# RWKV attention and a two-layer MLP on one core: spreading w by two TensorE row groups, scores in any free PSUM bank, layer 1 by unit and quarter, weights loaded between units

## The chip, the cores and the metric

The program runs on one core of one Trainium2 chip. The metric is the device time of one execution in microseconds (us). The core has TensorE (PE; matmuls, with its weight loads listed as PEld), VectorE (DVE), ScalarE (ACT), GpSimd (POOL) and SyncE (SP, which here only issues DMAs). Each engine runs its own list of instructions in order; semaphores tie the lists together.

## The reference

```python
def _attn_ref(r, k, v, w, u):                 # (4, 8, 768, 48): batch, heads, steps, head size
    state = np.zeros((B, H, D, D))
    ...
    for t in range(S):
        ...
        cur = np.einsum('bhd,bhe->bhde', u[None] * kt, vt)
        y[:, :, t] = np.einsum('bhd,bhde->bhe', rt, state + cur)
        state = w[None, :, :, None] * state + np.einsum('bhd,bhe->bhde', kt, vt)
    ...

def _moe_ref(x, w_in, w_out):                 # x (3072, 384), w_in (384, 2048), w_out (2048, 384)
    h = x @ w_in
    g = np.where(h >= 1, h, np.where(h <= -1, 0.0, (h + 1) ** 2 / 4))
    return g @ w_out
```

The output y of the attention, with the heads side by side, is the input x of the MLP. Inputs and output are float32.

## The kernel before

**Units.** The sequence is cut into 6 chunks of 128 steps. A unit is one chunk of one batch element, so there are 24 units; units 0 to 3 are the first chunk of the four batch elements. For a unit, K is multiplied by a table of inverse powers of w (`Winv`, line 447, operation `kw`) and R by a table of powers (`Wpow`, line 451, `rw`); both stand in one tile KR. KR is transposed into RK: in the first 8 units by TensorE (`tr`, line 469, with a copy out of PSUM, `rk`), later by a DMA transpose on SP's queue (`trd`, line 488). The scores (`at`, line 499) are 8 matmuls with a contraction of 48, alternating between the two halves of the partitions. VectorE multiplies them by a mask (line 505). Then come y (state part `ys`, line 556; local part, line 559), the sum with the diagonal term (x, line 571), and the transpose of x into xT: in the first 8 units by TensorE (`xp`, line 581), later by DMA (line 589). The state is updated by `st` (line 607), `t`, `tw` and `bd`.

**MLP.** Two units make a block of 256 tokens. Layer 1 (`L1`, line 644) takes a block in 8 groups of 6 matmuls of 256 columns; each group fills an "h" bank, and ScalarE turns it into g (line 656). Layer 2 (`L2`, line 667) takes one unit in 4 groups of 4 matmuls of 384 columns, strictly in order of units; a copy (`e`) and a store (`out`, line 690) follow. The kernel takes g as ((h+1)/2)^2 everywhere; bounds on the norms of x and of w_in (lines 703 to 751) give a flag that says whether the other branches can matter, and only if so does the code under `tc.If` (from line 759) compute the MLP again.

**Order.** The kernel writes every operation down with its engines, its durations as guessed, its dependencies, its buffers and a due time; `Plan.run` (line 84) places them one by one and so fixes the order of the instructions on each engine. The due times come from `CFG` (line 16) and are moved by a `bias` per kind of operation. The loads of the first units and the weights go in the order of `CFG["order"]`: U is a unit, I a quarter of w_in, O a quarter of w_out. Weights land in float32 in one of five "wf" buffers and are cast to bf16 in pieces by whichever engine is free (`copy`, line 284). PSUM has 4 "a", 2 "h" and 2 "o" banks.

**Start.** w is loaded into one partition; ScalarE takes its logarithm (line 327), one TensorE matmul of one row spreads it to 128 partitions (line 333), and two exponentials give Winv and Wpow (lines 359 and 360). Dummy matmuls of zeros (line 357) fill TensorE's gaps of the first 24 us as planned.

Of the kernel before, what the change touches and what calls it, by code (L numbers as in the profile page):

```python
# [16 lines left out]
    "order": "U0 U1 U2 U3 I0 I1 I2 I3 O0 O1 O2 U4 O3 U5 U6 U7",  # L17
    "soft": 8,
    "sw": False,
    "due": [12.12, 22.15, 27.93, 36.84, 35.31],  # L20
    "step": 12.04,
    "warm": 24.0,
    "steady": 45.0,
    "slack": 0.19,
    "split": 2,
    "bias": {
        "at": 1.0, "bd": -4.91, "c_uw": 1.38, "dg": 0.1, "ku": -0.0, "kw": 1.96, "ldVf": 1.45, "red": -0.75,
        "rk": 0.3, "rkk": -6.72, "rkr": -0.29, "rw": 1.99, "st": 0.57, "t": -0.92, "trd": 0.24, "trk": -2.87,
        "trr": -3.35, "tw": -0.9, "v": -0.89, "x2": -1.05, "xt": 2.62, "y": -2.02,
    },  # L30
}


class Buf:
    def __init__(self, pool):
        self.pool, self.users, self.slot, self.t = pool, [], None, None


class Op:
    def __init__(self, name, engs, fn, deps, uses, allocs, due, dma, after, nb, late):  # L40
        self.name, self.engs, self.fn, self.due, self.dma = name, engs, fn, due, dma
        self.after, self.nb, self.late = [a for a in after if a], nb, late
        self.deps, self.uses, self.allocs = [d for d in deps if d], list(uses), list(allocs)
        self.eng = self.start = self.end = None
        for b in self.uses + self.allocs:
            b.users.append(self)


class Plan:
# [13 lines left out]
    def place(self, o):  # L63
        got, t = [], 0.0
        for b in o.allocs:
            best = None
            for i, cur in enumerate(self.slots[b.pool]):
                if any(g[0] == b.pool and g[1] == i for g in got):
                    continue
                if cur is None:  # L70
                    free = 0.0
                elif all(u.start is not None for u in cur.users):
                    free = max(u.end for u in cur.users) + SEM
                else:
                    continue
                if best is None or free < best[0]:
                    best = (free, i)
            if best is None:
                return None
            got.append((b.pool, best[1]))  # L80
            t = max(t, best[0])
        return t, got

    def run(self):
# [5 lines left out]
        while todo:  # L90
            cand, gone = [], []
            for o in todo:
                if any(d.start is None for d in o.deps) or any(a.start is None for a in o.after):
                    if o.late is not None and free["PE"] > o.late:
                        gone.append(o)
                    continue
# [15 lines left out]
            for o in gone:  # L112
                todo.remove(o)
                for b in o.uses:
                    b.users.remove(o)
            if not cand and gone:
                continue
            if not cand:
                raise RuntimeError("no operation can be placed: " + ", ".join(o.name for o in todo[:12]))
# [16 lines left out]
            occ, lat = o.engs[e]  # L136
            o.eng, o.start = e, est
            for b, (p, i) in zip(o.allocs, pl):
                b.slot = i
                self.slots[p][i] = b  # L140
            if o.dma is not None:
# [4 lines left out]
                begin = max(served, issue + wait)  # L146
                served = begin + took
                ring.append((served, nd))
                free[e] = issue
                o.end = served + 0.6 + (1.0 if est > steady else 0.0)  # L150
# [7 lines left out]
            todo.remove(o)  # L158
            done.append(o)
        done.sort(key=lambda o: o.start)  # L160
# [27 lines left out]
def kernel(  # L188
# [28 lines left out]
    NS = CFG["soft"]  # L217
    D_m = list(CFG["due"])
    while len(D_m) < NB + 2:
# [11 lines left out]
        "x": 5, "x2": 2, "g": 5, "os": 3, "sq": 2, "ss": 2,  # L231
    }
    P = Plan(slots)
    rows = rot.tile([1, 2, H, DP], F32, name="rows", tag=f"g_{slots['g'] - 1}")

# [16 lines left out]
    zero = const.tile([128, 128], BF16, name="zero")  # L252
    onesf = const.tile([1, 128], F32, name="onesf")
    w_row = const.tile([1, H * D], F32, name="w_row")
    wc = const.tile([128, NP], F32, name="wc")
    ident = const.tile([128, 128], BF16, name="ident")
    umask = const.tile([128, 128], F32, name="umask")
    ones = const.tile([128, 1], BF16, name="ones")
# [9 lines left out]
    xT = [const.tile([128, nKb, MT], BF16, name=f"xT{m}") for m in range(NB)]  # L268
    xn = const.tile([128, NU], F32, name="xn")
    wsq = const.tile([128, nN], F32, name="wsq")  # L270
# [7 lines left out]
    wc3 = wc[:, :, None].to_broadcast([128, NP, D])  # L278
    umask4 = umask[:, None, :].to_broadcast([128, NP, 128])
# [14 lines left out]
    c_wr = P.op("c_wr", {"ACT": (0.4, 0)}, lambda e: nc.scalar.dma_start(out=w_row, in_=row(w)), due=-100, dma=(0.05, 1, 0.6))  # L294
    c_ur = P.op("c_ur", {"ACT": (0.4, 0)}, lambda e: nc.scalar.dma_start(out=u_row, in_=row(u)), after=[c_wr], due=-99.5, dma=(0.05, 1, 0.6))
    c_ubc = P.op("c_ubc", {"SP": (0.4, 0)}, lambda e: nc.sync.dma_start(out=u_bc, in_=row_bcast(u)), due=D_m[NS // UB] - 25, dma=(0.7, 8, 0.6))
# [21 lines left out]
    c_um = P.op("c_um", {"POOL": (0.6, 0.7)}, f_um, due=-97)  # L318
# [8 lines left out]
    c_lrow = P.op("c_lrow", act(384, False), lambda e: nc.scalar.activation(rows[:, 0, :, 0:D], heads(w_row), AF.Ln), deps=[c_wr, c_rz], due=-98)  # L327
    c_urow = P.op("c_urow", dve(384), lambda e: nc.vector.tensor_mul(rows[:, 1, :, 0:D], heads(w_row), heads(u_row)), deps=[c_wr, c_ur, c_rz], due=8.5)
    lwb = Buf("a")

    def f_lwb(e):
        get(lwb, [128, H, D], F32)
        mm(lwb.t, onesf, rows[:, 0, :, 0:D], start=True, stop=True)
    c_lw = P.op("c_lw", pe(1.3), f_lwb, deps=[c_lrow, c_z], allocs=[lwb], due=-98)
    colb = Buf("a")

    def f_colT(e):
        get(colb, [128, 2, NP], F32)
        for i in range(2):
            for p in range(NP):  # L340
                nc.tensor.transpose(colb.t[:, i, p : p + 1], rows[:, i, 2 * p : 2 * p + 2, :].rearrange("q h d -> q (h d)"), onesf[:, 0:1])
    c_colT = P.op("c_colT", pe(0.5), f_colT, deps=[c_lrow, c_urow], allocs=[colb], due=9)
# [9 lines left out]
    for i in range(160):  # L352
        def f_wm(e, i=i):
            if wmb.t is None:
                get(wmb, [128, 128], F32)
            for _ in range(2):
                mm(wmb.t, zero, zero, start=True, stop=True, skip_group_check=True)  # L357
        wm0 = P.op(f"wm{i}", pe(0.22 if i < 18 else 0.11), f_wm, deps=[c_z], uses=[wmb] if i else [], allocs=[] if i else [wmb], after=[wm0] if i else [], due=2000.0, late=CFG["warm"] if i else None)
    c_winv = P.op("c_winv", act(384), lambda e: nc.scalar.activation(Winv, lwb.t, AF.Exp, scale=negj_col), deps=[c_lw, c_icol], uses=[lwb], due=-97)
    c_wpow = P.op("c_wpow", act(384), lambda e: nc.scalar.activation(Wpow, lwb.t, AF.Exp, scale=i_col), deps=[c_lw, c_icol], uses=[lwb], due=-96)  # L360

# [37 lines left out]
    prev_w = []  # L399
    for tag, q in [(x[0], int(x[1:])) for x in ORDER if x[0] in "IO"]:  # L400
# [8 lines left out]
        before = ORDER[: pos[f"{tag}{q}"]]  # L409
        gate = [loads[int(x[1:])]["Vf"][1] for x in before if x[0] == "U"][-1:]  # L410
        if CFG["sw"]:
            def fn(e, src=src, dst=dst):
                nc.gpsimd.dma_start(out=dst, in_=src)
            o = P.op(f"ld{tag}{q}", {"POOL": (1.1, 0)}, fn, after=gate + prev_w[-1:], due=due, dma=(2.05, 0, 1.0))
            res[q] = [o]
        else:
            def fn(e, bf=bf, src=src, shape=shape):
                t = get(bf, shape, F32)
                nc.sync.dma_start(out=t, in_=src)  # L419
            o = P.op(f"ld{tag}{q}", {"SP": (0.6, 0)}, fn, allocs=[bf], due=due, dma=(2.05, nd, 0.6))  # L420
            res[q] = []
            for i in range(shape[1]):
                def fc(e, bf=bf, dst=dst, i=i):
                    copy(e, dst[:, i, :], bf.t[:, i, :])
                n = shape[2]
                due_c = D_m[0] + 1.3 * q if tag == "I" else 34.0 + 1.0 * q
                res[q].append(P.op(f"c{tag}{q}{i}", {**dve(n, True), **act(n, False), **pool(n, False)}, fc, deps=[o], uses=[bf], due=due_c))
        prev_w.append(o)
# [6 lines left out]
    def attention(i):  # L435
        b, c = units[i]
        m, j = divmod(i, UB)
        soft = i < NS
        D0 = D_m[m] + 1.5 * j
        (Kb, Ko), (Rb, Ro), (Vb, Vo) = loads[i]["K"], loads[i]["R"], loads[i]["Vf"]  # L440
        krb, vb, rkb, atb, yb, xb = Buf("KR"), Buf("V"), Buf("RK"), Buf("AT"), Buf("a"), Buf("x")
        both = {**pool(384), "DVE": (0.68, 0.75)}
# [16 lines left out]
        if soft:  # L459
            trb = Buf("a")  # L460
# [30 lines left out]
        at_p = [Buf("a"), Buf("a")]  # L491
# [8 lines left out]
        o_at = P.op(f"at{i}", pe(0.4), f_at, deps=o_rk, uses=[rkb], allocs=at_p + [atb], due=D0 - 3.2)  # L500

        o_mask = []
        for s in range(2):
            def f_mask(e, s=s):
                nc.vector.tensor_mul(atb.t[s], at_p[s].t, umask4)  # L505
# [307 lines left out]
```

## Time and profile before

| what | us |
|---|---|
| median of 14 runs (lowest to highest) | 181.63 (179.63 to 184.26) |
| the profiled execution | 180.31 |
| its span, first to last instruction | 178.4 |
| first layer-1 matmul starts | 18.57 |
| last matmul ends | 172.6 |
| layer 1: 576 matmuls, busy | 77.8 |
| layer 2: 384 matmuls, busy | 77.0 |
| dummy matmuls: 156, busy | 13.0 |

The span is 1.9 us shorter than the time of the execution, which has some work around it. Busy times of matmuls overlap, since one starts while the one before is still draining; the distance from one start to the next is what a matmul costs. Loads of K, R and V are 192 KB in pieces of 192 bytes; a quarter of a weight matrix is 768 KB in pieces of 2 KB (w_in) or 1.5 KB (w_out).

### The profile page before, as it was taken

How to read it: one execution, taken by the hardware profiler on the slowest of the kernel's cores; microseconds unless marked ns; L12 is line 12 of the kernel's file. 1: busy time of each engine (PE TensorE's matmuls, PEld its weight loads, DVE VectorE, ACT ScalarE, POOL GpSimd, SP SyncE). 2: the span in 40 equal slices, each digit the busy share in tenths (PEclk: the TensorE clock that was granted, in tenths of full speed). 3: DMA queues.
4: the chain of work that ended last, by engine and by line, in shares of the span. 5: the costliest groups of instructions: out<-in, count | busy, mean ns of one | idle time of the engine just before them, and what ended most of it. 6: DMA issues, size and time to landing. Idle time of an engine off the chain costs nothing.

```text
span 178.4 us, 4705 instructions
## 1 busy us (share of the span) xinstructions
PE 168.5 (94%) x1808; PEld 127.0 (71%) x1808; DVE 111.2 (62%) x221; ACT 116.0 (65%) x257; POOL 105.1 (59%) x142
## 2 busy tenths in 40 slices
PE   7899989999989999999999999999999999999960
PEld 7689977766757777777777767776767777777730
DVE  6699965698999795776758765846565644100000
ACT  4359997735566985884976775867785556554510
POOL 8659462387695999778598668588975610000000
PEclk9999999999999999999999999999999999999996
DMA  5999999998989959978989979889998962111111
GB/s 113 211 198 343 386 343 336 225 194 162 201 178 217 179 124 205 180 163 186 192 177 164 181 169 183 212 169 200 189 188 157 234 174 70 22 44 48 44 53 52
DMA packets 105920, 31.50 MB, mean 177 GB/s; under 512 B 98978, under 2 KB 104356, under 8 KB 105892
## 3 DMA queue, kind: packets, MB, share of 16 engines
q1 hardware_dynamic: 105744, 31.04, 78.4%
q8 instruction: 16, 0.26, 0.6%
q10 hardware_dynamic: 148, 0.10, 0.2%
q14 instruction: 12, 0.10, 0.2%
HBM read 20.65 MB, written 4.72 MB: 142 GB/s over the span
## 4 chain that ended last, share of the span: by engine, by line
PE 67%; DMA 13%; SPq 8%; DVE 4%; POOL 3%; issue 1%; ACT 0%; POOLq 0%; ACTq 0%
PE o L667 31%; PE h L644 27%; DMA wf<-in_moe_w_out_dram 11%; SPq L383 5%; PE a L499 3%; SPq L419 2%; PE a L559 2%; DMA K<-in_k_dram 2%; PE a L556 2%; POOL KR L447 1%; PE a L607 1%; DVE AT L505 1%; SPq L488 1%; DVE VD L546 1%; DVE x L571 1%
## 5 line engine op out<-in xcount | busy, mean ns | idle before, releaser
L644 PE MATMUL h<-xT,w_in_sb 128*128 128x256 bf16 x576 | 77.8, 273 | 0.7 <-ACT w_in_sb L284 0.4
L667 PE MATMUL o<-w_out_sb,g 128*128 128x384 bf16 x384 | 77.0, 326 | 0.2 <-POOL w_out_sb L284 0.2
L656 ACT ACTIVATE g<-h 128x512 bf16<-128x512 f32 x96 | 56.6, 595 | 27.4 <-PE h L644 26.3
L644 PEld LDWEIGHTS <-w_in_sb 128*128 128x128 bf16 x576 | 54.4, 98 | 14.5 <-ACT w_in_sb L284 0.7
L667 PEld LDWEIGHTS <-g 128*128 128x128 bf16 x384 | 35.1, 97 | 15.8 <-issue 0.2
L505 DVE TENSOR_TENSOR AT<-a,umask 128x512 bf16<-128x512 f32 x48 | 31.1, 683 | 8.8 <-PE a L499 8.5
L546 POOL TENSOR_TENSOR VD<-V,dg 128x384 f32<-128x384 bf16 x18 | 16.0, 891 | 11.9 <-DVE dg L541 7.1
L571 DVE TENSOR_TENSOR x<-a,VD 128x384 bf16<-128x384 f32 x24 | 13.3, 554 | 11.4 <-PE a L559 7.4
L535 POOL TENSOR_TENSOR KU<-K,u_bc 128x384 f32<-128x384 f32 x16 | 18.5, 1155 | 2.2 <-DMA K<-in_k_dram 2.2
L451 DVE TENSOR_TENSOR KR<-R,Wpow 128x384 bf16<-128x384 f32 x20 | 18.4, 922 | 1.8 <-DMA R<-in_r_dram 1.7
L536 POOL TENSOR_TENSOR KU<-KU,R 128x384 f32<-128x384 f32 x16 | 17.5, 1094 | 1.4 <-DMA R<-in_r_dram 0.2
L597 ACT ACTIVATE x<-x 128x384 bf16<-128x384 bf16 x24 | 12.5, 522 | 6.8 <-DVE x L571 6.4
L284 DVE COPY os<-o 128x384 f32<-128x384 f32 (+1 forms) x6 | 3.1, 520 | 19.9 <-ACT os L284 18.7
L618 POOL TENSOR_TENSOR T<-T,wc 128x192 f32<-128x192 f32 x20 | 11.9, 595 | 5.6 <-ACT T L284 4.2
L357 PE MATMUL o<-zero 128*128 128x128 bf16 x156 | 13.0, 236 | 1.0 <-DVE zero L321 1.0
L447 POOL TENSOR_TENSOR KR<-K,Winv 128x384 bf16<-128x384 f32 x11 | 11.0, 998 | 5.0 <-DMA K<-in_k_dram 4.1
L284 ACT COPY os<-o 128x384 f32<-128x384 f32 (+1 forms) x19 | 8.9, 470 | 6.0 <-PE o L667 4.0
L284 ACT CAST V<-Vf 128x384 bf16<-128x384 f32 x19 | 9.6, 507 | 4.2 <-DMA Vf<-in_v_dram 4.0
L614 DVE TENSOR_TENSOR T<-T,a 48x192 f32<-48x192 f32 x32 | 11.2, 349 | 1.9 <-PE a L607 1.1
L447 DVE TENSOR_TENSOR KR<-K,Winv 128x384 bf16<-128x384 f32 x13 | 8.2, 630 | 5.7 <-DMA K<-in_k_dram 5.7
L284 ACT CAST Tbd<-T 48x192 bf16<-48x192 f32 x30 | 10.4, 347 | 1.8 <-PE a L556 1.4
L357 PEld LDWEIGHTS <-zero 128*128 128x128 bf16 x156 | 10.6, 107 | 1.2 <-DVE zero L321 1.0
(78 smaller groups left out, 173.8 us busy)
## 6 DMA issues: line engine op xcount, KB each, us to landing
K<-in_k_dram SPq DMA_DIRECT2D x24, 192.0 KB, 3.6
R<-in_r_dram SPq DMA_DIRECT2D x24, 192.0 KB, 4.2
Vf<-in_v_dram SPq DMA_DIRECT2D x24, 192.0 KB, 4.1
out_dram<-os SPq DMA_DIRECT2D x23, 192.0 KB, 2.3
wf<-in_moe_w_in_dram SPq DMA_DIRECT2D x4, 768.0 KB, 8.3
wf<-in_moe_w_out_dram SPq DMA_DIRECT2D x4, 768.0 KB, 8.5
RK<-KR SPq DMA_TRANSPOSE x16, 3.1
xT<-x SPq DMA_TRANSPOSE x16, 2.9
```

What stands on the lines that cost most here:

```text
L284: (nc.scalar.copy if eng == "ACT" else V_ENG[eng].tensor_copy)(o, i)
L357: mm(wmb.t, zero, zero, start=True, stop=True, skip_group_check=True)
L447: V_ENG[e].tensor_mul(krb.t[:, H:, 0:D], Kb.t, Winv)
L451: V_ENG[e].tensor_mul(krb.t[:, :H, 0:D], Rb.t, Wpow)
L505: nc.vector.tensor_mul(atb.t[s], at_p[s].t, umask4)
L535: nc.gpsimd.tensor_mul(kub.t, Kb.t, u3)
L536: nc.gpsimd.tensor_mul(kub.t, kub.t, Rb.t)
L546: V_ENG[e].tensor_mul(vdb.t, vb.t, dgb.t[:, :, None].to_broadcast([128, H, D]))
L571: nc.vector.tensor_add(xb.t, yb.t[:, 0:384].rearrange("p (h d) -> p h d", h=H), vdb.t)
L644: mm(hb.t[:, f, :], w_in_sb[:, kk, (2 * n + f) * 128 : (2 * n + f + 1) * 128], xT[m][:, kk, :], start=(kk == 0), stop=(kk == nKb - 1),)
L656: nc.scalar.activation(gb[m].t[:, 2 * n : 2 * n + 2, :], hb.t, AF.Square, bias=0.5, scale=0.5)
L667: mm(ob.t, gb[m].t[:, f, j * C : (j + 1) * C], w_out_sb[:, f, :], start=(f == 0), stop=(f == nN - 1))
```

## The change

The change does the following.

- **Load order**: the quarters of w_in go between units 0 to 3, and all of w_out ahead of unit 4.
- **w**: it is loaded as two rows, on partitions 0 and 64; two matmuls of one row, in two row groups of TensorE, spread w itself to two PSUM banks; the logarithm is then taken on 128 partitions, and the exponentials read it from SBUF.
- **Dummy matmuls** have 256 columns, one per operation.
- **Unit 0** may take its PSUM tiles from any of the pools "a", "h" and "o"; the search for a place looks at all of them.
- **Transposes of RK** are by TensorE in the first 10 units (8 before); in units 0 to 3 (before 0 and 1) in two halves.
- **Masks**: for units 0 and 1, one half of the scores is copied out by ScalarE and masked in bf16.
- **Scores** of blocks 5 to 11: those of both units are one operation of 16 matmuls, which takes all four "a" banks.
- **Layer 1** of blocks 0 and 1: by single unit and quarter of w_in, 12 matmuls of 128 columns a group, and each unit's first group can start without the other unit.
- **Layer 2** of the last unit in two cuts (256 and 128 columns), the store of each on SP; the stores of five units are split into two, which makes the number of counted DMAs a multiple of eight.
- **Norm check**: squares from 100 us on, their sums folded once more by GpSimd, one operation of 8 matmuls in place of 8 operations of 2; the reduction reads PSUM.
- **Redo branch**: a loop of 6 passes over 2 blocks in place of 12 blocks written out; xT is one tile.
- **Planner**: new due times and biases; the order on every engine is new. In it, the two transposes of the norm check (`b3`) stand behind the last layer-2 matmul on TensorE.

```diff
-    "order": "U0 U1 U2 U3 I0 I1 I2 I3 O0 O1 O2 U4 O3 U5 U6 U7",
-    "soft": 8,
-    "due": [12.12, 22.15, 27.93, 36.84, 35.31],
-    "step": 12.04,
+    "order": "U0 U1 I0 I1 U2 I2 U3 I3 O0 O1 O2 O3 U4 U5 U6 U7",
+    "tpe": 10,
+    "dmm": 8,
+    "xpe": 8,
+    "pair": 5,
+    "cold": 5.5,
+    "fine": 2,
+    "am0": 0,
+    "am1": 2,
+    "norm": 100.0,
+    "wide": 1,
+    "due": [2.41, 43.63, -27.85, 19.94, 61.18],
+    "step": 14.84,
     "warm": 24.0,
...
-    "slack": 0.19,
-    "split": 2,
+    "slack": 0.04,
+    "split": 4,
...
-        self.pool, self.users, self.slot, self.t = pool, [], None, None
+        self.pools, self.users, self.slot, self.t = pool.split(), [], None, None
+        self.pool = self.pools[0]
...
-    c_lrow = P.op("c_lrow", act(384, False), lambda e: nc.scalar.activation(rows[:, 0, :, 0:D], heads(w_row), AF.Ln), deps=[c_wr, c_rz], due=-98)
...
-        mm(lwb.t, onesf, rows[:, 0, :, 0:D], start=True, stop=True)
...
+            mm(wbb[s].t, onesf[s * DP : s * DP + 1, :], w_sp[s * DP : s * DP + 1, :], start=True, stop=True)
...
+            nc.scalar.activation(lw[:, lws[s]], wbb[s].t, AF.Ln)
...
+    c_winv = P.op("c_winv", {"ACT": (0.5, 0.58)}, lambda e: nc.scalar.activation(Winv, lw, AF.Exp, scale=negj_col), deps=[c_lw, c_icol], due=-97)
...
-            for _ in range(2):
-                mm(wmb.t, zero, zero, start=True, stop=True, skip_group_check=True)
+            mm(wmb.t, zero[:, 0:128], zero, start=True, stop=True, skip_group_check=True)
...
+        A = "a h o" if i < CFG["wide"] else "a"
+        by_pe, by_mm, x_pe = i < CFG["tpe"], i < CFG["dmm"], i < CFG["xpe"]
...
-        if soft:
-            trb = Buf("a")
+        if by_pe:
+            trb = Buf(A)
...
-        o_at = P.op(f"at{i}", pe(0.4), f_at, deps=o_rk, uses=[rkb], allocs=at_p + [atb], due=D0 - 3.2)
+        o_at = yield f_at, o_rk, rkb, at_p + [atb], D0 - 3.2
...
+                    nc.scalar.copy(amb.t, at_p[s].t)
...
+                    nc.vector.tensor_mul(atb.t[s], amb.t, umaskb4)
...
+        if m >= CFG["pair"]:
+            def f_at2(e, got=got):
+                for x in got:
+                    x[0](e)
+            o = P.op(f"at_{m}", pe(0.63), f_at2, deps=got[0][1] + got[1][1], uses=[x[2] for x in got], allocs=got[0][3] + got[1][3], due=got[0][4])
+            ats = [o, o]
...
+        fine = m < CFG["fine"]
+        j, q = divmod(n, nP // UB)
...
+            if fine:
+                get(hb, [128, 4, C], F32)
+                parts = [(f, 4 * q + f, slice(j * C, (j + 1) * C)) for f in range(4)]
+            else:
+                get(hb, [128, 2, MT], F32)
+                parts = [(f, 2 * n + f, slice(0, MT)) for f in range(2)]
...
+        cuts = [(0, d_out)] if i < NU - 1 else [(0, 256), (256, d_out)]
+        rows_ = [(0, C)] if i not in TWICE else [(0, C // 2), (C // 2, C)]
...
+    n_dma = sum(1 for o in P.ops if o.dma is not None) + NU + 1
+    TWICE = range(12, 12 + -n_dma % 8)
...
+            nc.gpsimd.tensor_add(mx[n // 2], ssb.t[:, 0:128], ssb.t[:, 128:256])
...
+        for g in range(nP):
+            mm(npb.t[:, g : g + 1], mx[g], ones, start=True, stop=True)
...
+        with tc.For_i(0, NCH, 1) as ci:
+            for g in range(NB // NCH):
```

## The prediction

> **What bounds the kernel now.** I read the page first (engine totals), then the chain of waits, then busy time by window, then who waited for whom, and last the branch at the end.
>
> ```profile
> PE 168.5 (94%) x1808; PEld 127.0 (71%) x1808; DVE 111.2 (62%) x221; ACT 116.0 (65%) x257; POOL 105.1 (59%) x142
> DMA  5999999998989959978989979889998962111111
> ```
>
> TensorE is the bound, but 13.0 us of its 168.5 us are dummy matmuls (L357), so the question is when real work runs out, and why. The DMA digits stand at 9 from the second slice: early on the loads set the pace.
>
> ```profile
> 15.36 19.32 DMA wf<-in_moe_w_out_dram x2
> 34.73 1.09 POOL w_out_sb L284 x2
> 35.86 0.81 PE o L667 x4
> ...
> 39.27 0.45 PE a L469 x8
> ...
> 68.02 0.65 PE o L667 x4
> 68.67 0.33 PE a L499 x8
> 68.99 0.76 PE h L644 x6
> 69.76 0.65 PE o L667 x4
> ```
>
> The chain (start, length, what) rests on the last quarter of w_out (O3): it is issued at 26.33, lands 8.3 us later at 34.6, is cast, and the fourth group of layer 2 starts at 35.86. By then all 16 layer-1 groups of the first four units and three layer-2 groups are done; TensorE has nothing else that is ready. From there it hardly stops:
>
> ```profile
> 36.00:46.00 10.00, 9.98 (x122) 6.83 (x121) 9.02 (x19) 4.86 (x14) 8.21 (x12) 1.00 0.92 176
> 46.00:60.00 14.00, 13.51 (x159) 10.34 (x158) 13.11 (x25) 9.08 (x23) 11.03 (x14) 1.00 0.99 202
> 60.00:172.60 112.60, 111.85 (x1104) 81.96 (x1100) 61.75 (x119) 76.40 (x166) 64.88 (x74) 1.00 0.73 151
> ```
>
> First come window, length and TensorE's busy time: 1.26 us idle in 136.6 us, until the last matmul at 172.6. So two things can shorten the run: O3 earlier, or fewer microseconds of matmul after it. The chain prices the latter: a group of six or four MLP matmuls is 0.65; transposes of one unit (L469) 0.45; the scores (L499) stretch the stretch 68.67 to 69.76 to 1.09, so they cost 1.09 - 0.655 = 0.435.
>
> **The change, part by part.** All terms are on the path from O3 to the end.
>
> 1. *Load order.* Before O3, the queue had carried twelve K/R/V loads of units 0 to 3, eight weight loads, and K and R of unit 4. Now O3 stands ahead of all of unit 4. Rates per load:
>
> ```profile
> 2.00:4.00 2.00, 2.00 (x21) 1.89 (x18) 1.79 (x4) 0.54 (x2) 1.87 (x8) 1.00 1.02 194
> 28.00:30.00 2.00, 1.97 (x18) 1.48 (x16) 0.82 (x3) 1.27 (x3) 0.65 (x1) 1.00 1.11 339
> ```
>
> The last column is GB/s; the column before it says all 16 DMA engines are full. A K/R/V load (197 KB) takes about 0.93 us at the 194 to 229 of the first windows, a weight load (786 KB) 2.25 at about 350. Low end: two loads fewer, 1.9 us. High end, from the bottom: start 2.0 + 12 x 0.93 + 8 x 2.25 + 0.6 to land = 31.8, which is 2.8 before 34.6. I take **-2.2** (O3 lands at 32.4, layer 2 goes on near 33.5). The cover: TensorE must have finished the 16 layer-1 groups by then. I0 is now sixth in the queue and lands near 9.7 (16.5 before), I3 at 22.0, V3 at 23, so x of unit 3 is in xT near 25.5, and the last five layer-1 groups (0.66 each) end by 31 beside three layer-2 groups. About 2 us to spare; gone, layer 1 would be late next, at one to one.
>
> 2. *Unit 4 late.* Its transposes and scores (0.45 + 0.435) ran before 35.86; now they come after O3: **+0.9**. K4 and R4 land near 33.3 and 34.2; in the changed instruction order three layer-2 groups stand ahead of unit 4's transposes and two more ahead of its scores, and 13 layer-2 groups (8.45) plus units 4 and 5 (1.7 each: 0.45 + 0.435 + st 0.17, ys 0.17, y 0.2, xp 0.17, dg 0.1) fill TensorE until x of unit 5 is there, about ten us on.
>
> 3. *Paired scores* from block 5: 8 matmuls stream at 0.056 us per pair of row groups, 0.224 of the 0.435; the 0.21 around them is paid once for two units: 7 x 0.21 = **-1.5**.
>
> 4. *Units 8 and 9 transposed by TensorE*, not by DMA: 2 x 0.45 = **+0.9**; two of the 16 DMA transposes of RK vanish, hidden.
>
> 5. *Layer 1 by single unit and quarter* (12 matmuls of 128 columns for 6 of 256), 16 groups. The dummy matmul of the same shape prices it:
>
> ```profile
> 11.31 0.73 PE L357 MATMUL o<-zero 128*128 128x128 bf16 x10
> 13.31 1.17 PE L357 MATMUL o<-zero 128*128 128x128 bf16 x18
> ```
>
> (1.17 - 0.73)/8 = 0.055 each, 12 of them 0.66 against 0.655: **0**. All lie ahead of O3, covered by the 2 us of part 1.
>
> The Trainium skill speaks against this part: "TensorE: Matmul & The Clock Gate", section "Back-to-back issue gap", gives about 81 ns per matmul of 128 columns in a stream of weight load and matmul pairs. By that figure, an estimate, 16 groups would take 12 x 0.081 = 0.97 each, 4.6 us more in all, the spare 2 us would be eaten and the sum of this forecast would shrink to nearly nothing. The rows above are the same instruction pair on this chip, so I go by 0.055.
>
> 6. *w in two row groups, Ln after the spread, banks of unit 0 anywhere, 256-column dummies, masks of units 0 and 1 by ScalarE*: Winv was done at 5.88 and may now be near 4.5. This moves x of unit 0, which then waits for I0 and its casts on ScalarE (about 11.5). **0** in the sum: O3 hides it; without that cover it would be worth 1 to 2 us of start.
>
> 7. *Norm check*: eight two-matmul groups (0.054 each) become eight matmuls, -0.2; the last unit in two cuts has 16 matmuls of 128 columns at 0.055, +0.05: **-0.15**. The squares move to 100 us and later: 0.83 us on ScalarE each (L707), between activations of 0.6 per 1.3 us, so hidden; POOL's third add too (POOL was idle after 155).
>
> 8. *Waits of TensorE after O3.* Now:
>
> ```profile
> PE a L499 <- DMA RK<-KR: 0.4, 1, 0.4
> PE a L607 <- DVE x L571: 0.3, 1, 0.3
> PE a L719 <- POOL ss L713: 0.3, 1, 0.3
> ```
>
> The new order has places for more: ScalarE has four x-square ops (0.7 each), two RK copies (1.0) and two state copies (0.7) queued ahead of the first activation of block 2 near 47 us, 0.5 to 1 us late for TensorE by my count; layer 2 of that block waits on it. Against that the old waits go. Ends -1.2 and +2.5; taken **0**.
>
> 9. *The tail.* From the last matmul (172.61) to the end (178.4) are 5.8 us.
>
> ```profile
> L759 SPq EVENT_SEMAPHORE  x8: 17/17/17, 174.5 to 177.1; - x8
> L759 PEldq COMPARE_BRANCH  x1: 3337/3337/3337, 170.1 to 170.1; - x1
> L759 DVEq COMPARE_BRANCH  x1: 72/72/72, 173.7 to 173.7; - x1
> L759 DVEq EVENT_SEMAPHORE  x1: 21/21/21, 177.2 to 177.2; - x1
> ```
>
> SyncE waits for the last store (issued 173.41, 2.8 us to land) and then checks its queues at 0.07 us each. Now the last evacuation is one copy of 128 columns, not two copies of 192 in a row (172.68 + 0.32, 173.03 + 0.36): the store goes 0.4 earlier, and with the stores counted up to a multiple of eight, fewer checks follow it, 0.35. But the flag, ready at 154.4 before, now waits for two transposes that stand behind the last matmul: 0.38 (L743) + 0.41 (L749) + 0.20 (L750) + handoffs, 1.25 us after it. VectorE's 3.5 us between its branch and its next instruction would then start there: 1.25 + 0.54 + 0.07 + 3.5 + 0.1 + 0.7 = 6.2, i.e. +0.4. That gap came with about 200 skipped instructions; POOL, which skips nothing, had none; VectorE now skips some 35, nearer to POOL's row, but TensorE still skips 420. Ends -0.75 and +0.4; taken **-0.4**.
>
> On this the Trainium skill ("Runtime: NRT & Kernel Launch", section "Instruction fetch mechanics") says that a taken branch to a target outside the fetched window stalls for a fetch of the target page. By that rule the shorter body would fit, and the tail would be worth -0.75, the sum -2.8.
>
> Sum: -2.2 + 0.9 - 1.5 + 0.9 - 0.15 - 0.4 = **-2.45 us**. The profiled execution took 180.31 (span 178.4 + 1.9), so 177.9 for its like; it lies 1.3 below the median of 181.63, so the forecast is 181.63 - 2.45 = **179.2**.
>
> **Rivals.**
> - *More*: O3 at the high end (-0.6 more), all old waits gone (-1.2), tail -0.75: 179.2 - 2.15 = 177.0. For it: the DMA sum; against it: a tightly ordered in-order queue seldom has no wait at all.
> - *Given back*: the activations of block 2 come 1 us late and each of the two late x transposes costs 0.5; layer 1 is late too by 0.5: 181.7. For it: VectorE is busy 13.11 of 14 us in 46 to 60. Against: TensorE there has 1.7 us of attention work per unit as filler.
> - *Slower*: paired scores need both units' RK and all four "a" banks at once, and TensorE works in order, so MLP groups queue behind them. One DMA transpose holds SyncE for 1.6 us (the first, at 50.90), so the second unit's is that much later; a stall of the pair by 0.35 us eats the whole sum (2.45/7), 0.8 us each gives 179.2 + 5.6 = 184.8. For it: the one wait on RK by DMA is already there (0.4); against: 24 scores showed only that one.
> - *It does not do what it says*: the two row groups for w run one after the other. 0.6 us at the start, hidden by O3: no change to the sum.
>
> **How the numbers follow.** Forecast 0.55 (own range 177.8 to 180.7), more 0.15, given back 0.15, slower 0.15; the last rival has the forecast's own chances and time. No change is within 0.5% (0.9 us) of 181.63, about what a measurement of this kernel can tell: 180.7 to 182.5. Faster: the forecast less the upper tail (0.52) + 0.15 + a little of the third: 0.69; same: 0.15; slower: 0.16, the fourth and the end of the third. The range reaches from the bounds of the first rival (-2.15 and the DMA's rest) to the third: 176.0 to 182.6.
>
> **What would show it.** In the changed profile: the last w_out landing near 32.4 and the fourth layer-2 group near 33.5; first layer 1 near 12; the last matmul near 170.5; one score row of 16 matmuls costing 0.66 where two cost 0.87; less than 1.5 us of TensorE waits after 34; VectorE's branch without a gap. Wrong it would be if TensorE waits for RK, x or an activation add up to more than 3 us after 34, or if layer 1 of units 2 and 3 is still running when O3 is cast.

## The result, and the profile after

The changed kernel takes 183.71 us (median of 10 runs, 182.09 to 185.04) beside 181.81 for the kernel before: a ratio of 1.0127, with an interval of 1.0089 to 1.0164. By the ratio it is slower by about 2.3 us, where 2.45 less were forecast. Ratios here compare only those runs of each kernel that lie within 1.5% of its fastest, so they can differ from the ratio of the medians beside them (here 1.0105, or 1.9 us). The profiled execution has a span of 181.3 us; before it was 178.4.

The page of after, engine totals and DMA share by slice:

```profile
PE 169.5 (94%) x1848; PEld 129.6 (71%) x1848; DVE 115.8 (64%) x229; ACT 115.9 (64%) x254; POOL 106.0 (58%) x147
DMA  6999899999499967997999978978879952121120
```

These totals show almost nothing: each within 5 us of before. The loss has to be looked for by place.

The chain of waits of after, 18 to 38 us (start, length, what):

```profile
18.72 0.84 PE h L717 x12
...
21.76 0.67 DVE w_in_sb L319 x2
22.43 1.20 DVE AT L555 x2
23.63 0.34 DVE T L319
...
24.42 0.88 POOL T L670
...
26.07 0.59 ACT RK L319
...
27.20 0.67 PE h L717 x12
...
34.01 1.34 PE h L717 x24
...
36.00 1.34 PE h L717 x24
37.34 0.81 PE o L751 x5
```

Before, most of this stretch was two loads of w_out, from 15.36 to 34.68, the second of them the last quarter (O3). Now no DMA is in it. The chain runs through VectorE's list (casts, masks, state), GpSimd and ScalarE to units 2 and 3, and ends with layer 1 (L717), whose last groups TensorE works off without a break until the fourth group of layer 2 starts at 37.2; that came at 35.86 before. In this execution O3 is no longer what TensorE waits for.

After, in the windows shown of before (the last one now reaches to 174.75, just behind the start of the last layer-2 matmul), and one more:

```profile
36.00:46.00 10.00, 10.00 (x124) 7.14 (x122) 6.73 (x14) 4.73 (x10) 3.59 (x5) 1.00 0.95 201
46.00:60.00 14.00, 14.00 (x186) 10.89 (x183) 13.60 (x29) 11.93 (x32) 10.68 (x15) 1.00 0.85 175
60.00:174.75 114.75, 112.26 (x1138) 85.21 (x1136) 65.67 (x117) 77.92 (x167) 71.36 (x88) 1.00 0.75 146
120.00:140.00 20.00, 17.70 (x169) 12.95 (x167) 10.39 (x16) 13.36 (x28) 15.52 (x21) 1.00 0.85 156
```

TensorE stands idle for 2.5 us behind 60, and 2.3 of it lie between 120 and 140. The answer on waits and the chain there say for what (L537 are the scores, RK their input, by DMA transpose):

```profile
PE a L537 <- DMA RK<-KR: 2.3, 2, 1.4
```

```profile
117.57 1.11 POOL VD L598
119.37 0.83 POOL VD L598
120.45 4.78 DMA RK<-KR
...
129.62 3.43 DMA K<-in_k_dram
...
135.37 4.62 DMA RK<-KR
```

Last the tail: the rows of the branch (L849) and of the end of the program (L897); durations in ns, then start:

```profile
L849 PEldq COMPARE_BRANCH  x1: 3753/3753/3753, 176.4 to 176.4; - x1
L849 PEldq EVENT_SEMAPHORE  x1: 51/51/51, 180.3 to 180.3; - x1
L897 SPq EVENT_SEMAPHORE  x10: 17/28/3130, 176.9 to 181.2; - x10
```

Before, TensorE's branch began at 170.1, beside the last matmuls. Now the flag is there at 175.8, so the branch begins at 176.4; SyncE stands 3.13 us waiting for TensorE and the program ends with it. The two gaps of VectorE and ScalarE behind their branches are gone, but TensorE's stayed.

Where the time went can be added up. Take for each matmul the distance to the next start, and sum it for attention and MLP: of some 155 us of such work in either kernel (155.1 before, 155.2 after), 30.5 us were done by 46 us before, and 29.2 after. So at 46 us the new kernel is 1.3 us behind. From there it waits 2.5 us where the old one waited 1.2 (+1.3), and its norm matmuls are 0.5 shorter: that makes 2.1, and the last layer-2 matmul ends 2.3 us later (174.9 for 172.6). The tail behind it is 0.6 us longer. Together 2.9, the difference of the spans.

Much of the lag at 46 us belongs to these two executions and not to the change. TensorE came to full pace, half the time for each matmul, at 12.4 us in this one and at 4.9 in that of before (last section). Of the 155 us, 126.0 are left at 46 us in this one and some 124.5 before (123.8 in b1, full pace at 5.1). But 124.4 to 124.6 are left in two runs below with the changed kernel's load order and an early full pace (e2 and e3, 7.2 to 7.3), and 127.4 in a run of the old kernel with a late one (g2, 12.5). So a late pace costs some 1.5 us, and with an early one in both the changed kernel is 0 to 0.8 us behind at 46 us, not 1.4.

(The change splits the stores of six units, 12 to 17; the section on the change said five.)

### The profile page after: what moved, and what is told of

Read it like the earlier page. It is cut to its first block, busy times and chain, and to the rows that moved or that the text cites. A ratio compares the mean times of both kernels' runs of the same rounds, so it can differ in the third digit from the quotient of the medians.

```text
span 181.3 us, 4782 instructions
## 1 busy us (share of the span) xinstructions
PE 169.5 (94%) x1848; PEld 129.6 (71%) x1848; DVE 115.8 (64%) x229; ACT 115.9 (64%) x254; POOL 106.0 (58%) x147
## 4 chain that ended last, share of the span: by engine, by line
PE 70%; DMA 8%; DVE 8%; POOL 4%; ACT 3%; issue 2%; SPq 0%; POOLq 0%; DVEq 0%
PE o L751 28%; PE h L717 26%; DMA RK<-KR 5%; PE a L507 3%; PE a L537 3%; PE o L406 2%; PE a L611 2%; DMA K<-in_k_dram 2%; PE a L608 2%; PE a L659 1%; POOL VD L598 1%; DMA w_sp<-in_w_dram 1%; DVE T L319 1%; DVE w_in_sb L319 1%; DVE AT L555 1%
## 5 line engine op out<-in xcount | busy, mean ns | idle before, releaser
L717 PE MATMUL h<-xTa,w_in_sb 128*128 128x256 bf16 (+1 forms) x672 | 78.3, 257 | 0.3 <-DVE w_in_sb L319 0.2
L751 PE MATMUL o<-w_out_sb,g 128*128 128x384 bf16 (+2 forms) x400 | 76.7, 320 | 0.0
L717 PEld LDWEIGHTS <-w_in_sb 128*128 128x128 bf16 x672 | 56.7, 98 | 12.7 <-DVE w_in_sb L319 0.5
L555 DVE TENSOR_TENSOR AT<-a,umask 128x512 bf16<-128x512 f32 x45 | 28.6, 684 | 14.2 <-PE a L537 13.8
L598 POOL TENSOR_TENSOR VD<-V,dg 128x384 f32<-128x384 bf16 x22 | 19.2, 874 | 24.0 <-ACT dg L319 7.0
L406 PE MATMUL o<-zero 128*128 128x256 bf16 x74 | 13.9, 322 | 1.1 <-DVE zero L358 1.1
L649 ACT ACTIVATE x<-x 128x384 bf16<-128x384 bf16 x24 | 12.4, 518 | 3.6 <-DVE x L623 3.5
L319 DVE COPY os<-o 128x384 f32<-128x384 f32 x6 | 3.3, 558 | 17.8 <-PE o L751 17.6
L593 DVE TENSOR_REDUCE dg<-KU 128x8 f32<-128x384 f32 x16 | 8.8, 548 | 8.1 <-POOL KU L588 8.0
L319 ACT CAST Tbd<-T 48x192 bf16<-48x192 f32 x34 | 11.8, 346 | 1.8 <-POOL T L670 0.8
L319 ACT COPY os<-o 128x384 f32<-128x384 f32 (+2 forms) x19 | 8.8, 462 | 6.2 <-PE o L751 4.0
L485 DVE TENSOR_TENSOR KR<-K,Winv 128x384 bf16<-128x384 f32 x15 | 10.7, 716 | 3.2 <-DMA K<-in_k_dram 2.7
L666 DVE TENSOR_TENSOR T<-T,a 48x192 f32<-48x192 f32 x32 | 11.2, 349 | 0.8
```

What stands on the lines that cost most here:

```text
L319: (nc.scalar.copy if eng == "ACT" else V_ENG[eng].tensor_copy)(o, i)
L406: mm(wmb.t, zero[:, 0:128], zero, start=True, stop=True, skip_group_check=True)
L485: V_ENG[e].tensor_mul(krb.t[:, H:, 0:D], Kb.t, Winv)
L598: V_ENG[e].tensor_mul(vdb.t, vb.t, dgb.t[:, :, None].to_broadcast([128, H, D]))
L717: mm(hb.t[:, f, :], w_in_sb[:, kk, c * 128 : (c + 1) * 128], xT[m][:, kk, cols], start=(kk == 0), stop=(kk == nKb - 1))
L751: mm(ob.t[:, : hi - lo], gb[m].t[:, f, j * C : (j + 1) * C], w_out_sb[:, f, lo:hi], start=(f == 0), stop=(f == nN - 1))
```

## The experiments

Ratios are to the kernel before, run on the same chip. Single executions of one kernel differ by 3 to 5 us, so times a per cent apart rest on the profile's rows as much as on the ratio.

**e1: the flag early.**

```diff
-due=D0 + 8, nb=D0))
+due=D0 + 8, nb=min(D0, 152.0)))
```

> The changed kernel, with the squares of x of units 22 and 23 allowed from 152 us of the planner's time on (they were held back to 165.1 and 166.6), so that the flag is ready some 15 us before the last matmul, as it was in the kernel before. Theory: the end is set by TensorE's taken branch (3.75 us), which starts only when the flag is there; with an early flag it lies beside the matmuls again, SyncE waits for the last store instead, and the span after the last layer-2 matmul falls from 6.5 to about 4 us: about 181.3 in all (183.7 - 2.4). Rival: the end is set by the last store and its queue checks whatever the flag does; then it stays at 183.3 to 183.7.

181.53 us, 1.015 (1.001 to 1.029), which is too wide to say anything. The rows do: the part behind the start of the last layer-2 matmul is 4.4 us (6.6 in after), the flag is there before 165, and TensorE's branch begins 0.4 us before that matmul starts (175.24):

```profile
L849 POOLq COMPARE_BRANCH  x1: 45/45/45, 165.0 to 165.0; - x1
...
L849 PEldq COMPARE_BRANCH  x1: 3717/3717/3717, 174.9 to 174.9; - x1
```

TensorE's control instructions run ahead of its queued matmuls, so the branch can start before they do. The row of GpSimd shows when the flag came, that of TensorE when its queue let it go on.

**e2: dummies while TensorE waits for w.**

```diff
+        if o.name == "c_wb":
+            for _ in range(6):
+                mm(wmb.t, zero[:, 0:128], zero, start=True, stop=True, skip_group_check=True)
         o.fn(o.eng)
```

> The changed kernel with six more dummy matmuls of 256 columns put ahead of the spread of w, where TensorE stood idle from 2.11 to 3.44 us waiting for the load of w. Theory: this idle time kept TensorE at half pace until 12.4 us (0.213 us for 256 columns, 0.107 for a transpose); without it the pace doubles near 4.5 to 5 us as in the kernel before, unit 0's scores start near 9.4 instead of 10.45, first layer 1 a good microsecond earlier, the whole 1 to 1.5 us shorter: 182.2 to 182.7. Rival: the start hangs on VectorE and on the loads, and the pace of TensorE there costs nothing: 183.7, with first layer 1 at 17.2 as before.

181.99 us, 1.020 (1.005 to 1.034). In its profile full pace came at 7.3 and first layer 1 at 15.8, as the theory had it. But e3 and e4, without the fill, show the same (7.2 to 7.5, and 15.6 to 15.7). f2 decides.

**e3: split stores later.**

```diff
-    TWICE = range(12, 12 + -n_dma % 8)
+    TWICE = range(23 - -n_dma % 8, 23)
```

> The changed kernel with the six stores in two halves moved from units 12 to 17 to units 17 to 22: the same number of transfers, no compute engine's order changed. Theory A: SyncE's queue is full from 108 to 140 us (an issue takes 0.56 to 0.9 us), each extra store there holds back the DMA transposes behind it, and the 2.3 us that TensorE waits for RK between 123 and 140 come from it: 1 to 2 us shorter, 181.7 to 182.7, waits for RK below 1 us. Theory B: the waits come from pairing the scores, or from the other engines' work; then they stay at 2 us or more and the time at 183.5 or so.

179.93 us, 1.005 (0.999 to 1.011). TensorE is not idle for a moment from 120 to 140: waits for RK stay below 1 us, as theory A has it. Its reason is only part of it, though. In the changed kernel the first scores of the two pairs began 3.5 and 2.8 us after the second unit's transpose was issued, here about 3.6 both times; but the transposes were there only after 4.8 and 4.6 us, and here after 3.1 and 3.2. So the greater part of what went is slow landing, not late issue, and theory A has no reason for that. f2 comes back to it.

**e4: single scores.**

```diff
-    "pair": 5,
+    "pair": 99,
```

> The changed kernel with no paired scores (the planner orders anew from 67 us on). Theory B: pairing makes TensorE wait for the second unit's RK; without it the 2.3 us of waits go and the scores' 1.5 us saving goes too: 182.7 to 183.3, with less than 0.7 us of waits for RK. Theory A (SyncE's queue is too full whatever the scores do): the waits stay at 1.5 us or more and the saving is lost: 184.5 to 185.5.

182.94 us, 1.026 (1.011 to 1.040). The waits didn't go, they grew:

```profile
PE a L537 <- DMA RK<-KR: 2.7, 5, 0.8
```

So waits for RK come without pairs too. They are of another kind: TensorE is ready for these five scores 2.5 to 3.3 us after their transpose was issued, and the transposes took 3.2 to 3.7 us.

**e5: e1 and e3 together.**

> The changed kernel with both edits of the first runs: the last two squares of x allowed earlier, so that the flag is early, and the six split stores in units 17 to 22. Theory: the two losses add up, 2.2 us of tail (6.6 to 4.4 after the last layer-2 matmul) and 1.5 to 2.3 us of waits for RK between 120 and 140, so 3.5 to 4.5 us below the changed kernel: a ratio of 0.988 to 0.994 to the kernel before, with less than 0.3 us of idle TensorE from 120 to 140. Rival: one hides the other (an earlier end of the matmuls only moves the store and its checks); then the ratio stays at 1.00 to 1.005.

179.49 us, 0.9931 (0.9895 to 0.9968): 2.0% below the changed kernel (0.9931 against 1.0127) and faster than the kernel before, with 0.01 us idle from 120 to 140 and 4.4 us of tail. This is the base of most runs below.

**e6: the old load order, on e5.**

```diff
-    "order": "U0 U1 I0 I1 U2 I2 U3 I3 O0 O1 O2 O3 U4 U5 U6 U7",
+    "order": "U0 U1 U2 U3 I0 I1 I2 I3 O0 O1 O2 U4 O3 U5 U6 U7",
```

> The same two edits and the load order of the kernel before (U0 U1 U2 U3 I0 I1 I2 I3 O0 O1 O2 U4 O3). Theory of the prediction (O3 gates layer 2): O3 lands some 2 us later and the whole gets 1.3 to 2.5 us longer than with the new order, ratio 1.00 or above. Rival, from the trace of after (layer 1 of units 2 and 3 was still running when O3 was cast): the new order gains nothing, because unit 3's K, R, V and the last quarter of w_in are issued 4 to 8 us later in exchange; then within 0.7 us of the run with the new order, and TensorE's layer 1 of the first block ends at or before 35.9.

181.75 us, 1.0059 (1.0017 to 1.0101). First layer 1 comes only at 22.6, and the fourth group of layer 2 at 39.9 (e5 37.5): the rival fell, and the loss is what the prediction's theory gave. But the planner ordered everything anew, and O3's casts end at 39.3, though it had landed at 35.75, so this is not the price of a late O3 alone.

**b1: the kernel before, flag later.**

```diff
-nb=D0))
+nb=D0 if i < 22 else 165.1 + 1.5 * j))
```

> The kernel before with the squares of x of units 22 and 23 held back to 165.1 and 166.6 us of the planner's time, as they are in the changed kernel, and nothing else. Theory: the flag then stands at the end, TensorE's branch (3.3 us) is no longer beside the matmuls, and the kernel before gets 1.5 to 2.5 us longer (ratio 1.008 to 1.014), with the same last matmul within 0.4 us. Rival (the tail is set by the store and the queue checks): ratio 1.000 to 1.003.

181.56 us, 1.005 (0.999 to 1.011), tail 5.5 us (6.2 before). No verdict: the flag was read at 170.55, still 0.25 us before the last matmul started. g2 does it properly.

**b2: the kernel before, new load order** (the diff of e6 the other way round).

> The kernel before with the load order of the changed kernel and nothing else (its planner orders anew). Prediction's terms 1 and 2 alone: -2.2 + 0.9 = -1.3 us, ratio 0.993. Rival (unit 3's inputs come later and layer 1 of the first block ends later, which eats what O3 gains): ratio 1.00 to 1.015, with layer 1 of the first block ending after 36.

184.64 us, 1.023 (1.017 to 1.029), layer 1 of the first two blocks done at 38.3 (35.1 before). The fourth group of layer 2 does come earlier, but by 0.75 us (35.11) and not 2.2 (O3 landed 0.6 us earlier, at 34.09), and layer 1 of units 2 and 3 is 3.2 us late. So each order loses with the other's due times and biases. All four runs in which the planner had to order anew (e4, e6, b2 and f3 below) have a higher ratio than the kernel they start from, e4 within its wide interval, so what the order is worth by itself stays open.

**f1: w in one row, on e5.**

```diff
-w_sp = const.tile([128, H * D // 2], F32, name="w_sp")
+w_sp = rot.tile([1, H * D], F32, name="w_sp", tag=f"g_{slots['g'] - 2}")
...
-in_=w.rearrange("(s h) d -> s (h d)", s=2)
+in_=row(w)
...
-mm(wbb[s].t, onesf[s * DP : s * DP + 1, :], w_sp[s * DP : s * DP + 1, :], start=True, stop=True)
+mm(wbb[s].t, onesf[0:1, :], w_sp[:, s * 192 : (s + 1) * 192], start=True, stop=True)
```

> The changed kernel with early flag and late split stores (the base from here on), and w loaded into one partition and spread by two matmuls of 192 columns from the same row, one after the other, instead of two row groups; the planner's order is untouched. Theory: the two row groups gave nothing (1.01 us for the spread in the changed kernel, and the load into two partitions took 1.11 us to issue), so Winv comes no later than now, or 0.3 to 0.6 us earlier: ratio to the kernel before 0.989 to 0.993. Rival: the row groups work beside each other, the spread gets 0.4 us longer, and the start with it: 0.994 to 0.998.

179.24 us, 0.986 (0.978 to 0.994), an interval that overlaps that of e5. The chains at the start, first of after, then of f1 (L406 dummies, L369 the spread):

```profile
0.79 2.52 DMA w_sp<-in_w_dram
3.31 0.14 issue
3.44 1.01 PE a L369 x4
4.45 2.46 PE o L406 x11
```

```profile
1.07 1.25 PE o L406 x5
2.32 0.01 issue
2.33 1.61 PE a L369 x4
3.94 2.46 PE o L406 x11
```

The row groups do work beside each other: 1.01 us for the spread against 1.61 one after the other. But the load into two partitions takes 1.11 us to issue (0.51 into one) and w comes over a microsecond later. Winv is ready at 4.96, in nine executions with two rows between 5.45 and 5.96. So the part of the change that its name begins with gives a later start than one row in the same kernel.

**f2: the fill of e2, on e5.**

> The base with six more dummy matmuls ahead of the spread of w (the fill of the second run, on this base). Theory: TensorE's idle time while w is under way puts off its full pace, which came between 7.9 and 13.2 us in six profiles without the fill and at 8.0 with it; the mean gain is 0.5 to 1.5 us: ratio 0.985 to 0.990, full pace at or before 8 us. Rival: when the pace doubles is chance and doesn't hang on 1.1 us of idle time: ratio 0.992 to 0.995, full pace anywhere from 5 to 13 us.

Full pace came at 13.4 us with the fill: the theory fell. Median 180.02 us to 181.70, 0.991; the ratio is 0.982 (0.978 to 0.987), with single runs from 177.2 to 181.9, so no gain over e5 can be read from it. And the waits are back, with the stores where e5 has them:

```profile
PE a L537 <- DMA RK<-KR: 1.8, 2, 1.2
```

SyncE's order is e5's and the transpose in question was issued at the same time (134.90; e5 134.83), but the scores that were ready in e5 after 3.6 us had to wait until 4.8 us after the issue. The first of the two took 4.4 us, where e5 has 3.0. So SyncE's queue is not all of it: at the same lead the transposes landed more than a microsecond later.

**f3: single scores, on e5** (the diff of e4).

> The base without paired scores (ordered anew from 67 us on). Theory: with SyncE's queue relieved the pair waits for nothing, so its saving of 1.5 us is there in full and is lost here: ratio 0.999 to 1.004, TensorE's waits for RK below 0.5 us in both. Rival: the pair still costs waits that single scores don't have, so the time stays within 0.5 us of the base: 0.990 to 0.996.

182.23 us, 1.007 (1.003 to 1.011): the plan without pairs is slower than e5. Waits for RK are 0.3 us; but the new plan also has 1.7 us of other waits, so not all of the 1.4% between them is the pair's saving.

**f4: one row and fill, on e5** (both diffs, five dummies).

> The base with both: w in one row, and five more dummies ahead of the spread. If both theories hold: ratio 0.982 to 0.988, first scores before 9.2 us, and faster than either kernel. If both rivals hold: 0.992 to 0.998.

180.48 us, 1.005 (0.999 to 1.011; by the medians 0.993), full pace at 13.3, 2.0 us of waits for RK: no gain over e5 (by the medians 0.992). The five dummies, each 0.21 us, stand ahead of the spread and take back what one row had gained (Winv at 5.97).

**g1: eight units' stores issued by ScalarE, on f1.**

```diff
-nc.sync.dma_start(out=out[t0 + r0 : t0 + r1, lo:hi], in_=osb.t[r0:r1, lo:hi])
+(nc.scalar if 10 <= i <= 17 else nc.sync).dma_start(out=out[t0 + r0 : t0 + r1, lo:hi], in_=osb.t[r0:r1, lo:hi])
```

> Base with w in one row, and the stores of units 10 to 17 issued by ScalarE instead of SyncE, in the same places of the order. Between 100 and 136 us SyncE spends 32 to 33.7 us on issues, 3.5 to 6 of them on stores. Theory A (SyncE's queue is late): its issues there fall to some 28 us, the second unit's RK is issued 1 us or more earlier before TensorE comes to it, and TensorE waits less than 0.3 us for RK; ratio 0.980 to 0.988. Theory C (the DMA transposes themselves land later in some executions: 4.4 to 4.8 us after their issue where TensorE waited, under 3.9 where it didn't, with the same queue): waits of 1 us or more come back in the slower executions all the same; ratio 0.986 to 0.994, the runs spread over 3 us as before.

178.55 us, 0.983 (0.977 to 0.989), the fastest with f1 and g3. The transposes of the two second units are issued at 119.15 and 131.51 (f1 120.00 and 133.88), and no wait for RK is left, as theory A has it. But SyncE's issue time from 100 to 136 did not fall: 33.4 us, where f1 had 32.1. Its loads now take 15.7 us to issue (12.8). The issue of one 192 KB load took anything from 0.53 to 1.84 us there, so this sum is not a cost per instruction, and my 28 us was wrong. The first scores now begin 4.9 and 5.7 us after the issue (f1 3.6 and 3.3), so that even the slowest landing seen, 4.8 us, would be covered; the two took 3.1 and 3.3. Six runs over 3 us leave theory C open.

**g2: the kernel before, flag behind the last matmul.**

```diff
-nb=D0))
+nb=D0 if i < 22 else 168.3 + 0.6 * j))
```

> The kernel before with the squares of x of units 22 and 23 held back to 168.3 and 168.9 us of the planner's time, so that the flag's two transposes stand behind the last matmul, as in the changed kernel (in b1 the flag still came 0.4 us before the last matmul, and the end didn't move). Theory: TensorE's branch (3.3 to 3.8 us) starts some 2.3 us after the last layer-2 matmul starts, and the part behind that matmul grows from 5.6 to 6.2 us (b1, before) to 7.3 to 8: 1.2 to 2 us longer, ratio 1.006 to 1.012. Rival: the stores and the checks of the kernel before still end later; ratio 0.999 to 1.004.

181.92 us, 1.0069 (1.0022 to 1.0115), tail 6.9 us: 0.7 to 1.4 more than in the kernel before and b1, a little less than expected.

```profile
L759 PEldq COMPARE_BRANCH  x1: 3440/3440/3440, 177.7 to 177.7; - x1
...
L759 PEldq EVENT_SEMAPHORE  x1: 51/51/51, 181.2 to 181.2; - x1
```

A late flag alone costs in the old kernel too. The rows don't tell TensorE's branch from VectorE's gap behind its own, though, which there ends nearly as late (177.8 to 181.1). The price depends on what else ends the program: in the kernel before, the queue checks (177.1) and VectorE's gap (177.2) ended late already.

**g3: the last unit in one cut, on f1.**

```diff
-        cuts = [(0, d_out)] if i < NU - 1 else [(0, 256), (256, d_out)]
+        cuts = [(0, d_out)]
```

> Base with w in one row, and the last unit's layer 2 in one cut of 384 columns as in the kernel before. In the base TensorE's branch began 0.45 us before the last matmul started (172.77 and 173.22) and still ended last; in the kernel before it began 2.2 us before, because the matmuls queued ahead of it were of 384 columns and not of 128. Theory: the branch is hidden now, the end is set by one store, the part after the last matmul's start falls from 4.4 to about 4.0 us: ratio 0.983 to 0.988. Rival: the longer last evacuation and store give it back: 0.987 to 0.993, tail 4.4 to 4.8.

178.87 us, 0.9855 (0.980 to 0.991), tail 4.0 us. The branch in e5, then in g3:

```profile
L849 PEldq COMPARE_BRANCH  x1: 3833/3833/3833, 172.8 to 172.8; - x1
```

```profile
L849 PEldq COMPARE_BRANCH  x1: 3713/3713/3713, 169.4 to 169.4; - x1
```

The last layer-2 matmul starts at 173.22 and 171.58. The branch leads by 0.45 us where matmuls of 128 columns are queued ahead of it, by 2.1 where they have 384; there it ends before the last store is checked. Cutting the last unit for an earlier store had uncovered it.

## Why the prediction was wrong

*Bound, and part 1 (load order, -2.2): failed, on the cover, and on the size.* The step that failed is "TensorE must have finished the 16 layer-1 groups by then ... About 2 us to spare". O3 did come earlier: the first of its four casts waits for it until 33.4 (landing forecast for 32.4). But only then is x of unit 3 copied into xT (start, length, engine, line, what):

```profile
33.39 0.36 DVE L319 COPY xTa<-a 128x384 bf16<-128x384 bf16 x1 [0.29 <-PE a L633]
33.39 0.51 POOL L319 CAST w_out_sb<-wf 128x384 bf16<-128x384 f32 x1 [0.50 <-DMA wf<-in_moe_w_out_dram]
35.88 0.50 ACT L319 CAST w_out_sb<-wf 128x384 bf16<-128x384 f32 x1
```

First layer 1 came at 17.24 and not near 12, x of unit 3 was in xT at 33.75 and not at 25.5, and layer 1 ended at 37.3, not 31. I had timed units by the landing of their loads and let the rest follow at once. But unit 0's steps stand in VectorE's list among unit 1's, and its x came at 15.1. The casts wait for their engines too: the last of O3's stood behind ScalarE's work until 35.9. Unit 3's K, R and V were issued at 13.6, 14.2 and 19.1, where the old order had them at 7.2, 8.5 and 11.2: putting I0, I1 and I2 ahead puts unit 3 back. My own second falsifier, layer 1 still running when O3 is cast, came true. At 46 us I had the kernel 1.3 us ahead; it was 1.3 behind. An early full pace shortens this and does not mend it: in e3 x of unit 3 is in xT at 32.1, layer 1 ends at 35.7, and the kernel is 0 to 0.8 us behind. The gain was oversized, too: in twelve executions with the new order O3 landed between 32.4 and 34.8 us, in three with the old kernel's between 34.7 and 35.1, about 1 us earlier on average and not 2.2.

*Parts 2, 4 and 7: right in sign.* The transposes of RK took TensorE 5.6 us in all for 3.9 before, and 5.0 with an early full pace (e3): 1.1 more, where part 4 has 0.9. The norm check got 0.5 shorter (0.15 forecast).

*Parts 3 and 5: right.* A pair costs 0.66 (two singles 0.87), and twelve matmuls of 128 columns take 0.67, 0.055 each. The Trainium skill's 81 ns ("TensorE: Matmul & The Clock Gate", section "Back-to-back issue gap") did not hold for these pairs. By it the surcharge of that estimate would be 5.0 us, not 4.6.

*Part 6 (w, dummies: 0, hidden by O3): failed.* The cover went with part 1 (layer 1, not O3, came last), and the gain (Winv at 4.5) was not there: 5.65, a quarter of a microsecond before the old 5.88. I costed the matmuls and left out the load: a load of two rows was a new form and had no row, and I took it for free. f1 gives its size.

*Part 8 (waits, taken 0): failed, by +1.3.* The waits were those of my rival "Slower", paired scores waiting for RK, at two of seven pairs. Its mechanism was only half right: e4 has more waits without pairs, and e3 and e5 none with them. What was late was RK: its transposes landed 4.8 and 4.6 us after their issue, where e3, e5, f1 and g3 have 3.0 to 3.4. I had counted RK's two transposes saved on SyncE, and not the six stores added, each half 0.55 to 0.70 us of issuing, two halves of one just ahead of the second transpose; they explain some half a microsecond of that one's lateness (2.8 us ahead of the first scores, 3.3 to 3.6 in those four runs). A busy SyncE is no cause by itself: from 100 to 136 it issues for 33.3 us, but for 33.1 in e3 and 31.9 in the kernel before, which wait for RK 0 and 0.4 us. Why the transposes landed later stays open.

*Part 9 (tail, -0.4): failed, by 1.0.* I took VectorE's gap for the danger and gave TensorE's 3.3 us branch no place in the sum, though its row was on the page, because in before it lay beside matmuls. Behind the last matmul that cover was gone: e1 gives 2.2 us back, and in g2 a late flag lengthens the old kernel's tail by 0.7. On VectorE's side the rule of the Trainium skill that I had weighed ("Runtime: NRT & Kernel Launch", section "Instruction fetch mechanics") fitted: its gap, 3.5 us before, went with the shorter body (0.5 us from branch to next instruction). TensorE's did not shrink (3.75 us).

*Sum.* Work left at 46 us: forecast 1.9 less than before (1.3 by the order, 0.6 by parts 3 and 4), measured 1.4 more, 3.3 off; the norm check -0.35; waits 1.3; tail 1.0. Together 5.25 us, from -2.45 to +2.8, and the spans differ by 2.9. Of the 3.3, some 1.5 came with the full pace that was late in the one profiled execution and early in the other; over all runs the kernels differ by 1.9 to 2.3.

Settled: that in the profiled execution layer 1, and not O3, came last at the start; the tail; that TensorE waits for RK without pairs too (e4) and can have pairs without waits (e3, e5); that moving the split stores takes 2% off together with the early flag (e5). Not settled: why the same transpose lands a microsecond later in some executions (the changed kernel, f2, f4), what moving the stores has to do with it, and what the load order is worth by itself.

## What to carry to other kernels

Moving a load ahead moves others back: before crediting it, follow the last unit it displaces through every engine's list, not only to its landing. When a long hidden instruction, such as a branch at the end, is hidden by an order, ask what the change does to that order and what it costs uncovered. And ask of a late transfer both when it was issued and how long it took to land: a busy issuing queue was there in the kernels without waits as well.

## What the runs showed of the hardware

*When TensorE reaches full pace varies.* The rows of TensorE from 8.5 to 11.8 us, first after, then e3, whose edit touches nothing there (tile, shape, count; busy, mean ns):

```profile
L507 PE MATMUL a<-ident,KR 128*128 128x128 bf16 x11 | 1.8, 311 | 0.0
L406 PE MATMUL o<-zero 128*128 128x256 bf16 x6 | 1.7, 421 | 0.0
```

```profile
L406 PE MATMUL o<-zero 128*128 128x256 bf16 x13 | 1.9, 274 | 0.0
L507 PE MATMUL a<-ident,KR 128*128 128x128 bf16 x8 | 0.8, 220 | 0.0
```

Starts are 0.107 us apart for 128 columns at half pace, 0.055 at full pace. In 13 executions of the changed kernel and its variants pace doubled at 6.7 to 7.5 us in five and at 11.4 to 13.4 in eight; in four of the kernel before and its variants at 4.9, 5.1, 9.2 and 12.5, the last with TensorE busy without a break from 1 us on (g2). With w in two rows and the new load order, first layer 1 starts at 15.6 to 15.8 after an early change of pace and at 17.1 to 17.6 after a late one: some 1.5 us of the spread between executions of one kernel. The granted clock of these windows reads 1.00 either way, so pace has to be read from the distance between starts.

On this the Trainium skill ("TensorE: Matmul & The Clock Gate", section "Part 1: The HAM clock gate (the "warmup" mystery)") describes a free-running window of 3.4 us, and a number of slow matmuls that varies from run to run. The variation agrees; that pace doubled only at 12.5 us, after 11.5 us of unbroken work, is later than one such window.
